# Masking the scale of Relu by expert, one sum for both halves, and turning the combine weights earlier

## The chip, the cores and the metric

The kernel runs on one core of a Trainium2 chip. The metric is the device time of one execution in microseconds (us), lower is better; a profiled execution has a span, and its time is a little longer than the span.

## The reference

An attention with a learned relative bias feeds a soft mixture of experts. Cut to what matters (the bias only named):

```python
# attention: 8 batches, 8 heads, 576 positions, head size 64, bias from a small MLP of log distances
attn = softmax(q @ k.T / 8 + bias) @ v            # -> x: 4608 tokens x 512
# soft MoE: 8 experts, 4 slots each (32 slots), hidden size 1024
logits = x @ phi                                  # 4608 x 32
d = softmax(logits, axis=tokens)
slot_input = (d.T @ x).reshape(8, 4, 512)
for e in range(8):
    slot_out[e] = relu(slot_input[e] @ w1[e]) @ w2[e]
c = softmax(logits, axis=slots)
out = c @ slot_out                                # 4608 x 512
```

## The kernel before, in words

**Main part.** 32 units (4 head pairs x 8 batches) go through attention. The order in which all steps are issued on all engines is a list written out by hand, `ORDER`: a token such as `Z/31` is step Z of unit 31. Each engine runs its own instructions in that order; semaphores make it wait for other engines. In the last eight units (24 to 31, one for each batch) each batch is also dispatched to the slots. Steps near the end of the list that matter here: `W` turns the exponentials and `wc` copies them into `ek`; `Z` multiplies them with the tokens (line 776) and `zc` (line 782) adds that to `accs`, the sums of all slots; `dq` copies the logits out of PSUM; `C`, `cA`, `cB`, `cC` make the combine weights of a batch, which are kept in `ck`; `F2` (line 826) and `F3` gather earlier sums. `cB/30` and `cB/31` are the two exponentials at line 750.

**The tail.** When the list is done, the code below `with tc.manual_schedule()` runs in program order. `turn_slots` transposes `accs` (line 971) and copies it to `sT` (line 973). `first(j)`, j = 0 to 7, multiplies it with w1 (line 986): Q = j // 4 is a half of four experts, which lie in four groups of 32 partitions, and within a group all 32 slots are computed, of which four are the expert's own. `hidden(Q)` applies Relu with the scale `stS` (1 / sum of the softmax), `turn_hidden(Q)` transposes the result to `hT` (line 1000). `stack(q)` transposes the combine weights of four batches to `cT` (line 1012) and those of the last 64 positions to `cR` (line 1015). `second(k, Q)` multiplies with w2 (line 1030) for k, one of four columns of 128 outputs. `gather_slots(k)` picks each expert's own four slots with the 0/1 matrix `sel`, one product for each Q (line 1042), and copies them to `sst` (line 1046). `put(k, q)` and `put_rest(k)` multiply with the combine weights (line 1063), copy the result from PSUM with ACT and DVE at once (line 377, tiles `ob`) and send it out (lines 1072 and 1079).

**PSUM.** There are eight banks. `Banks(w, n)` takes one bank (w = 1) or an aligned pair (w = 2) and gives it back after n calls of `read`, in program order: a pair is the one given back longest ago; a single bank is by preference one whose neighbour is taken, then the one given back longest ago. The new owner's products then wait for the old owner's copies. Each `put` and `put_rest` takes two pairs.

**Transfers.** All go through SP's queue in program order. `refetch` loads w2 tiles (512 KB each) into space that `first` has read.

## Time and profile before

| | |
|---|---|
| median of three runs | 580.82 us (578.47 to 581.24) |
| profiled execution | 579.62 us, span 577.8 us |
| PE, DVE, ACT, POOL busy | 547.1, 453.5, 458.4, 217.8 us |
| mean granted TensorE clock | 0.991 |
| HBM read, written | 81.25 MB, 27.41 MB |
| weight transfers | 62 of 512 KB (and 4 of 256 KB) |
| output transfers | 16 of 512 KB, 4 of 256 KB |

Busy times are of one core over the whole span. The lines of the profile have L and a line number of the kernel; `out<-in` are its tiles. Lines of the chain have start, length, engine and work; lines of the timeline add, in brackets, how long the engine had idled and who released it.

### The profile page before, as it was taken

How to read it: one execution, taken by the hardware profiler on the slowest of the kernel's cores; microseconds unless marked ns; L12 is line 12 of the kernel's file. 1: busy time of each engine (PE TensorE's matmuls, PEld its weight loads, DVE VectorE, ACT ScalarE, POOL GpSimd, SP SyncE). 2: the span in 40 equal slices, each digit the busy share in tenths (PEclk: the TensorE clock that was granted, in tenths of full speed). 3: DMA queues.
4: the chain of work that ended last, by engine and by line, in shares of the span. 5: the costliest groups of instructions: out<-in, count | busy, mean ns of one | idle time of the engine just before them, and what ended most of it. 6: DMA issues, size and time to landing. Idle time of an engine off the chain costs nothing.

```text
span 577.8 us, 19444 instructions
## 1 busy us (share of the span) xinstructions
PE 547.1 (95%) x7435; PEld 355.3 (61%) x7435; DVE 453.5 (78%) x1806; ACT 458.4 (79%) x955; POOL 217.8 (38%) x308
## 2 busy tenths in 40 slices
PE   5989899999999999999999999999999999989983
PEld 3445566667766666666776666667665666643762
DVE  7998778778889788787788888888897889862333
ACT  6979899988888998988988889888879788531233
POOL 4000445555545545555545544555334333400000
PEclk9999799999999999999999999999999999999998
DMA  5598613154865253868423256531453443699988
GB/s 159 213 310 297 187 64 105 62 161 143 294 182 188 90 177 120 288 190 290 157 88 102 85 187 170 179 104 43 137 186 123 124 169 118 245 392 408 404 336 329
DMA packets 43869, 109.91 MB, mean 190 GB/s; under 512 B 8448, under 2 KB 8576, under 8 KB 43776
## 3 DMA queue, kind: packets, MB, share of 16 engines
q1 hardware_dynamic: 43776, 108.67, 54.4%
q8 instruction: 58, 0.95, 0.7%
q14 instruction: 35, 0.29, 0.2%
HBM read 81.25 MB, written 27.41 MB: 188 GB/s over the span
## 4 chain that ended last, share of the span: by engine, by line
PE 67%; DVE 10%; ACT 9%; DMA 5%; issue 4%; POOL 2%; SPq 1%; DVEq 0%; ACTq 0%; POOLq 0%
PE ps L439 18%; PE ps L547 16%; PE ps L423 14%; DVE y L459 5%; ACT y L468 4%; PE ps L444 3%; DMA xo<-xs 3%; PE ps L557 3%; PE ps L1030 3%; PE ps L911 3%; PE ps L986 2%; ACT f L900 2%; POOL y L374 2%; DMA bias_m<-e 2%; ACT e L921 1%
## 5 line engine op out<-in xcount | busy, mean ns | idle before, releaser
L374 POOL TENSOR_SCALAR y<-y,sm 128x576 f32<-128x576 f32 x288 | 210.4, 746 | 274.1 <-DVE sm L476 218.3
L468 ACT ACTIVATE y<-y,mn 128x576 f32<-128x576 f32 x288 | 220.8, 770 | 21.2 <-DVE mn L459 16.0
L439 PE MATMUL ps<-qk 64*128 64x288 f32 x1024 | 161.1, 424 | 0.7 <-DVE ck L739 0.3
L377 ACT COPY at<-ps 128x1024 f32<-128x1024 f32 (+2 forms) x151 | 132.1, 895 | 22.1 <-PE ps L423 18.0
L547 PE MATMUL ps<-at,v 128*64 128x320 f32 (+1 forms) x1024 | 133.7, 410 | 0.2 <-ACT y L468 0.2
L459 DVE CUSTOM_DVE_ANT_0 y<-ps,bm,mn 128x288 f32<-128x288 f32 x256 | 123.4, 512 | 8.7 <-PE ps L439 3.4
L423 PEld LDWEIGHTS ps<-ident,y 64*128 64x128 f32 x2592 | 100.2, 139 | 43.4 <-POOL y L374 17.7
L459 DVE CUSTOM_DVE_ANT_0 y<-ps,bm 128x288 f32<-128x288 f32 x256 | 108.2, 453 | 15.1 <-PE ps L439 8.9
L423 PE MATMUL ps<-ident,y 64*128 64x64 f32 x2592 | 113.5, 227 | 3.3 <-DVE mn L459 1.0
L439 PEld LDWEIGHTS ps<-qk 64*128 64x128 f32 x1024 | 100.9, 188 | 18.6 <-DVE mn L459 3.2
L547 PEld LDWEIGHTS ps<-at,v 128*64 128x64 f32 x1024 | 69.9, 137 | 54.5 <-DVE mn L459 6.5
L468 ACT ACTIVATION_READ_ACCUMULATOR y<-y,mn 128x1 f32 x288 | 54.8, 190 | 0.0
L475 DVE TENSOR_SCALAR sm<-sm 128x2 f32<-128x2 f32 x144 | 36.2, 251 | 20.7 <-ACT y L468 20.3
L911 PE MATMUL ps<-f,wbd 128*32 128x79 f32 (+44 forms) x640 | 44.0, 404 | 6.8 <-DVE f L902 4.0
L902 DVE TENSOR_SCALAR f<-tabs,scl,nb 128x560 f32<-128x560 f32 (+17 forms) x106 | 45.9, 506 | 3.1 <-ACT f L900 1.5
L459 DVE DVE_READ_ACCUMULATOR2_ANT mn<- 128x1 f32 x576 | 47.6, 83 | 0.0
L911 PEld LDWEIGHTS ps<-f,wbd 128*32 128x32 f32 x640 | 22.0, 113 | 29.2 <-issue 10.5
L377 DVE COPY at<-ps 128x1024 f32<-128x1024 f32 (+2 forms) x41 | 31.2, 763 | 5.5 <-PE ps L423 4.4
L900 ACT ACTIVATE f<-tabs,cols,scl 128x432 f32<-128x432 f32 (+15 forms) x38 | 26.4, 748 | 2.5 <-DMA bias_m<-e 2.5
L476 DVE RECIPROCAL sm<-sm 128x2 f32<-128x2 f32 x144 | 23.8, 166 | 4.9
L921 ACT ACTIVATE e<-ps,bcon 128x591 f32<-128x591 f32 x36 | 25.8, 762 | 1.1 <-PE ps L911 1.1
L557 PE MATMUL ps<-at,v 64*64 64x320 f32 x128 | 23.9, 448 | 0.0
(150 smaller groups left out, 433.1 us busy)
## 6 DMA issues: line engine op xcount, KB each, us to landing
wt<-in_moe_w_dram SPq DMA_DIRECT2D x62, 512.0 KB, 6.9
qk<-in_qk_dram SPq DMA_DIRECT2D x32, 576.0 KB, 4.0
bias_m<-e SPq DMA_DIRECT2D x32, 295.5 KB, 3.6
v<-in_v_dram SPq DMA_DIRECT2D x32, 288.0 KB, 4.4
out_dram<-ob SPq DMA_DIRECT2D x16, 512.0 KB, 4.0
xs<-xts SPq DMA_DIRECT2D x24, 288.0 KB, 3.6
xo<-xs SPq DMA_DIRECT2D x8, 864.0 KB, 5.1
bm<-bias_m SPq DMA_DIRECT2D x16, 288.0 KB, 4.2
```

Of the source, the lines that this page charges most:

```text
L374: nc.gpsimd.tensor_scalar(out=out, in0=y, scalar1=r, scalar2=1.0, op0=ALU.mult, op1=ALU.mult)
L377: (nc.vector.tensor_copy if eng else nc.scalar.copy)(out=out, in_=in_)
L423: nc.tensor.matmul(out, src[rs], ident[rs, rs], is_transpose=True, start=True, stop=True, tile_position=(64 * r, 0))
L439: nc.tensor.matmul(pss[hh].t[:, 0:HALF], x[rs, S + p * P:S + (p + 1) * P], x[rs, k0:k0 + HALF], start=True, stop=True, tile_position=(64 * ...
L459: nc.vector.tensor_tensor_reduce(out=d["y", p][:, hs], in0=d["ps", p, n][hh].read()[:, 0:HALF], in1=biases[hp][p][:, hs], scale=-QS, scala ...
L468: nc.scalar.activation(out=y, in_=y, func=AF.Exp, bias=d["mn", p][:, 2 + hh:3 + hh], scale=-1.0, accum_out=d["sm", p][:, hh:hh + 1])
L475: nc.vector.tensor_scalar(out=r, in0=r, scalar1=1e-9, scalar2=None, op0=ALU.add)
L547: nc.tensor.matmul(po.t[o:o + 64, 0:wide[c]], d["v"][:, 64 * (4 * hh + i):64 * (4 * hh + i) + 64], main[:, :, 4 * hh + i, :], start=i == 0 ...
L557: nc.tensor.matmul(d["po", c].t[o:o + 64, 0:wide[c]], d["v"][rs, 512:576], keys[c][rs], start=False, stop=True, tile_position=(64 * hh, o))
L900: nc.scalar.activation(out=f, in_=tabs[:, 0:n], func=AF.Relu, bias=cols[:, 1:2], scale=sc)
L902: nc.vector.tensor_scalar(out=f, in0=tabs[:, 0:n], scalar1=sc, scalar2=nb1[:, 0:1], op0=ALU.mult, op1=ALU.max)
L911: nc.tensor.matmul(pb.t[32 * t:32 * t + 32, a // 512, a % 512:a % 512 + c1 - c0], wbd, x, start=True, stop=True, tile_position=(0, 32 * t))
```

## The change

- `turn_slots` makes `own`: `stS` times a 0/1 column for each Q, which is 1 where a row is a slot of the expert of its group. `hidden` uses it as Relu's scale, so that all other rows become 0.
- `second(k, 0)` and `second(k, 1)` then add into the same PSUM sums, and DVE copies them once for each k. `sel` loses its two halves, and `gather_slots` has one product.
- The sums and the gathered slots get a pair of banks of their own (`Banks(2, 99)`), one bank each, and are never given back. The gathered slots go into the second half of `so`.
- `stack` becomes a function of a list of batches. Six batches are turned as steps `k0/31` and `k1/31` in the list, ahead of and behind `Z/31`, and the last two behind `first(0)`. Each takes a single bank, and all copies are ACT's. `cT` is now two tiles.
- `second(k + 2, 0)` is written at the end of the loop, which is the same order as before.

The list gains two tokens; the rest of its diff is line breaks:

```diff
-... J8/30 F2/30 Z/31 F3/30 cC/31 d3/31 wat0/31 wqk0/31 wxo/31 zc/31 cB/30 wxk/31 cC/30
+... J8/30 F2/30 k0/31+ Z/31 k1/31+ F3/30 cC/31 d3/31 wat0/31 wqk0/31 wxo/31 zc/31 cB/30 wxk/31 cC/30
```

The rest:

```diff
-        sel = ends["sel"] = xp.tile([P, 2, P], F32, name="sel", tag="et2")
-        for Q in range(2):
-            nc.vector.tensor_scalar(out=sel[:, Q]..., scalar1=rowm[:, Q:Q + 1], ...)
+        sel = ends["sel"] = xp.tile([P, P], F32, name="sel", tag="et2")
+        nc.vector.tensor_copy(out=sel..., in_=rsum.unsqueeze(1).to_broadcast([P, 4, 32]))
+        own = ends["own"] = smp.tile([P, 2], F32, name="own", tag="se")
+        nc.vector.tensor_scalar(out=own, in0=rowm, scalar1=stS, scalar2=None, op0=ALU.mult)
...
-        nc.scalar.activation(out=hS[:, 0], in_=ends["h", Q].read()[:, 0], func=AF.Relu, scale=stS)
+        nc.scalar.activation(out=hS[:, 0], in_=ends["h", Q].read()[:, 0], func=AF.Relu, scale=ends["own"][:, Q:Q + 1])
...
+    def stack(turned, small):
+        if "cT" not in ends:
+            ends["cT"] = [xp.tile([P, 5, P], F32, name="cT", tag="lp")]
+        elif len(ends["cT"]) == 1:
+            ends["cT"].append(xp.tile([P, 5, P], F32, name="cT", tag="et"))
+            ends["cR"] = xp.tile([P, 2, 64], F32, name="cR", tag="acc")
+        h = Banks(1)
+        n = len(turned) * P
+        for i, b in enumerate(turned):
+            nc.tensor.transpose(out=h.t[:, i * P:(i + 1) * P], in_=ck[:, b, 0:4]..., identity=ident)
+        for q in small:
+            for i in range(4):
+                nc.tensor.matmul(h.t[32 * i:32 * i + 32, n:n + 64], ck[0:64, 4 * q + i, 4, :], ident[0:64, 0:64], ...)
+        h.read()
+        nc.scalar.copy(out=cT(turned[0], len(turned)), in_=h.t[:, 0:n]...)
+        for q in small:
+            nc.scalar.copy(out=ends["cR"][:, q], in_=h.t[:, n:n + 64])
+    step(U - 1, "k0", lambda _: stack((0, 1, 2, 3), ()))
+    step(U - 1, "k1", lambda _: stack((4, 5), (0,)))
...
     def second(k, Q, parts=(0, 1)):
-        if Q == 0:
-            ends["o", k] = Banks(1, 2)
+        if k == Q == 0:
+            ends["o"] = Banks(2, 99)
...
-        po = ends["o", k].t[:, P * Q:P * Q + P]
+        po = ends["o"].t[:, 0, P * k:P * k + P]
...
-                                     start=fq == 0 and x == 0, stop=fq == 1 and x == 3, tile_position=(0, 32 * g))
-        if parts[-1] == 1:
-            ends["o", k].read()
-            cp(Q == 0, ends["so"][:, Q, P * k:P * k + P], po)
+                                     start=Q == 0 and fq == 0 and x == 0, stop=Q == 1 and fq == 1 and x == 3,
+                                     tile_position=(0, 32 * g))
+        if Q == 1 and parts[-1] == 1:
+            nc.vector.tensor_copy(out=ends["so"][:, 0, P * k:P * k + P], in_=po)
     def gather_slots(k):
-        h = Banks(1)
-        pf = h.t[:, 0:P]
+        pf = ends["o"].t[:, 1, P * k:P * k + P]
         cs = slice(P * k, P * k + P)
-        for Q in range(2):
-            nc.tensor.matmul(pf, ends["sel"][:, Q], ends["so"][:, Q, cs], start=Q == 0, stop=Q == 1)
...
-        nc.scalar.copy(out=ends["sst"][:, cs], in_=pf)
+        nc.tensor.matmul(pf, ends["sel"], ends["so"][:, 0, cs], start=True, stop=True)
+        nc.scalar.copy(out=ends["so"][:, 1, cs], in_=pf)
...
         for j in range(4):
             first(j)
+            if j == 0:
+                stack((6, 7), (1,))
             refetch(*range(4 * j, 4 * j + (4 if j < 3 else 2)))
...
         turn_hidden(1)
-        stack(0)
-        second(0, 1)
-        stack(1)
+        second(0, 1, (0,))
+        second(0, 1, (1,))
+        second(1, 0)
         for k in range(4):
-            if k < 3:
-                second(k + 1, 0)
             gather_slots(k)
...
             put_rest(k)
+            if k < 2:
+                second(k + 2, 0)
```

## The prediction

> **What bounds the kernel now.** I read the page first, then stretches of the tail (the table of busy times by window), then the chain that ended last, and then the single rows of the tail in the timeline and the sync queue. The tail is where the edit lies, so the first question is what sets its end.

> ```profile
> span 577.8 us, 19444 instructions
> DMA  5598613154865253868423256531453443699988
> ...
> 502.00:554.60 52.60, 48.56 (x812) 28.13 (x807) 20.93 (x56) 13.56 (x33) 0.00 (x0) 1.00 1.01 397
> 554.60:557.00 2.40, 2.40 (x46) 1.71 (x46) 1.22 (x1) 1.28 (x2) 0.00 (x0) 1.00 0.34 126
> 557.00:562.60 5.60, 4.87 (x120) 3.60 (x112) 1.85 (x3) 1.55 (x3) 0.00 (x0) 1.00 1.02 398
> 562.60:565.00 2.40, 2.40 (x50) 1.85 (x48) 1.23 (x1) 1.30 (x3) 0.00 (x0) 1.00 0.22 82
> 565.00:576.60 11.60, 3.84 (x38) 1.96 (x30) 4.24 (x5) 3.74 (x6) 0.00 (x0) 0.92 1.01 398
> ```

> The columns after the stretch are PE, PEld, DVE, ACT and POOL busy, then the PE clock, the DMA share and GB/s. From 502 the DMA engines run full at about 398 GB/s, first on expert weights, then on outputs, with two holes: 2.40 us at 126 GB/s and 2.40 us at 82. Filled, they would save 2.40 x (1 - 126/398) = 1.64 and 2.40 x (1 - 82/398) = 1.91 us, 3.55 together. That is all this tail can give, because nothing ahead of k0 changes and no byte is taken away: 0.61% of the run. 0.5% is 2.9 us, about what a measurement of this kernel can tell from no change.

> ```profile
> 547.78 3.54 SPq L1072 DMA_DIRECT2D out_dram<-ob  x4
> 556.08 2.93 SPq L1072 DMA_DIRECT2D out_dram<-ob  x4
> 563.94 2.93 SPq L1072 DMA_DIRECT2D out_dram<-ob  x4
> 569.33 3.31 SPq L1072 DMA_DIRECT2D out_dram<-ob  x4
> ...
> out_dram<-ob SPq DMA_DIRECT2D x1, 512.0 KB, 2.6
> ```

> These are the first output issues of columns k = 0 to 3 in the sync queue, and (last line) the issue at 563.94, which lands 2.6 us later: 1.3 us of data, so 1.3 us ahead of it. The holes end when the outputs of k = 1 (556.08) and k = 2 (563.94) reach the queue. So the end of the kernel follows the issue of k = 2, and that follows TensorE, which the chain shows working back to back:

> ```profile
> 518.25 1.48 PE ps L776 x40
> 519.75 0.36 DVE accs L782
> 520.15 0.34 PE ps L971
> 520.51 0.27 ACT sT L973
> 520.83 10.51 PE ps L986 x96
> ...
> 537.68 1.02 PE ps L1000 x8
> 538.71 0.44 PE ps L1012 x4
> 539.14 0.24 PE ps L1015 x8
> ...
> 541.27 0.59 PE ps L1012 x4
> 541.86 0.25 PE ps L1015 x8
> ...
> 543.99 0.64 PE ps L1042 x4
> ```

> What counts is by how much later or earlier each put starts. I add shifts along this chain.

> **The change, part by part.**

> *The masked scale, sel and own.* The two Relu instructions keep their shapes and read another scalar column. The smaller sel and the new own are DVE work under the 10.51 us of first products, which need neither. Cost nothing; without that cover, well under 1 us.

> *k0 (turning four batches, ahead of Z/31).* By the rule of Banks (a lone bank whose neighbour is taken goes first) I followed the list by hand. F2/30 holds bank 3; k0 gets bank 2, which W/31 had; Z/31, which had it from W/31 before, now gets it from k0.

> ```profile
> 517.23 0.43 PE L826 MATMUL ps<-acc,rsum 128*32 128x128 f32 x8
> 517.65 0.56 ACT L750 ACTIVATE ck<-ck 128x160 f32<-128x160 f32 x2
> 517.77 0.33 DVE L377 COPY ek<-ps 128x160 f32<-128x160 f32 x1 [0.66 <-ACT xk L377]
> 538.30 0.59 ACT L377 COPY hT<-ps 128x512 f32<-128x512 f32 x1 [2.40 <-PE ps L1000]
> ```

> PE is idle from 517.66 to 518.25, which looks like room for the four transposes. But bank 2 is free only when the ek copy ends at 518.10; Z started 0.15 behind it. Now k0 starts there: four transposes 0.59 (to 518.84), a handoff of 0.02, the ACT copy of 128x512 (row: 0.59, to 519.45), 0.05 back, and Z at 519.50 instead of 518.25. **+1.25**. Lower end 0 (Z finds another bank and k0 fills the idle time), upper 1.5.

> *k1 (two batches and a quarter of rests, behind Z/31).* PE has it free while DVE adds accs, but ACT runs in order: k1's two copies and then cB/30, which ran at 517.9 before, now stand ahead of the copy of sT on which all first products wait.

> ```profile
> L377 ACT COPY ob<-ps 128x256 f32<-128x256 f32 x3 | 1.1, 378 | 0.0
> L1018 ACT COPY cR<-ps 128x64 f32<-128x64 f32 x2 | 0.4, 212 | 1.1 <-PE ps L1015 0.6 <-DVE hT L377 0.6
> ```

> Counted from the end of Z: two transposes (half of 0.59) and the small products (0.25) 0.55, handoff 0.02, copies 0.38 and 0.21, cB/30 0.28 (half of 0.56), sT 0.27, handoff 0.05: 1.76. Before it was 520.83 - 519.73 = 1.10. **+0.66**, between 0 and 0.9. The queue behind cB/30 on DVE (cC/30, four small operations) still ends under the first products.

> *stack((6, 7), (1,)) behind first(0).* Its weights are ready by then. Half of 0.59 and 0.25 on PE: **+0.55** (0.46 by the shorter row). The copies lie beside first products.

> *The old stacks leave.* The first took 0.44 + 0.24 = 0.69, but it covered ACT's copy of hT: that ends at 538.89, and the products that it feeds could start at 538.94, 0.23 behind the transposes. So 0.23 comes back as a wait: **-0.45**. The second took 0.84. It also kept column 1's sums, which now use the same bank, away from DVE's copy of column 0's:

> ```profile
> 537.80 0.29 DVE L377 COPY so<-ps 128x128 f32<-128x128 f32 x1 [1.05 <-PE ps L1030]
> 514.83 0.63 ACT L377 COPY lp<-ps 32x576 f32<-32x576 f32 x1 [4.41 <-DVE mb L657]
> ...
> 514.04 0.77 DVE mb L657
> ```

> No row shows PE writing a bank while another engine copies other columns of it. The nearest is dq/31 (second line): ACT needs nothing from DVE's minimum of the same banks, and yet idled 4.41 us and began 0.02 us after that had ended (514.81). So I let column 1 wait: 0.12 (537.68 to 537.80) + 0.29 + 0.05 = 0.46, and **-0.84 + 0.46 = -0.38**; the lower end is -0.84.

> [...]

> *One gather product instead of two.* Half of 0.64, four times: **-0.32** each, ahead of each put. The accumulation over Q costs no product; one copy of sums less per column was off the path.

> Sum at put(0, 0): 1.25 + 0.66 + 0.55 - 0.45 - 0.38 - 0.32 = **+1.31**.

> *The two own banks.* Before, second(2), second(3) and the last gather waited for a bank that an ACT copy was emptying:

> ```profile
> 549.05 0.40 PE L1063 MATMUL ps<-cR,sst 32*128 32x128 f32 x8
> 550.33 0.32 PE L1030 MATMUL ps<-wt,hT 128*32 128x128 f32 x4 [0.88 <-ACT ob L377]
> 558.19 0.43 PE L1030 MATMUL ps<-wt,hT 128*32 128x128 f32 x8 [0.73 <-ACT ob L377]
> ```

> That wait looks like the gain of the change, about 1 us a column. But two banks are now held to the end and three pairs are left. Followed by hand, put(k, 0) takes pairs A and B, put(k, 1) C and A, put_rest(k) B and C. Before, put_rest's second half had the pair of the sums and ran at once (0.40 for all eight). Now it needs C, which ACT is still emptying of put(k, 1): the same copy, the same end. PE is in order, so second(k+2) stands behind the same wait and behind half of put_rest: 0.20 later. I take **+0.20 per column**, not -1; the other end is a rival. With the gather's -0.32 each further column gains 0.12: put(1, 0) is at +1.19, put(2, 0) at **+1.07**.

> *What it meets in the queues.*

> ```profile
> SPq L882 <- PE ps L986: 2.9, 3, 2.2
> 541.32 0.33 SPq L882 DMA_DIRECT2D wt<-in_moe_w_dram  x1
> wt<-in_moe_w_dram SPq DMA_DIRECT2D x1, 512.0 KB, 10.1
> ```

> SP stops for first(0) to free weight space, 2.2 us at longest; first(0) ends 1.9 later, so 4.1. Transfers in flight last 10.1 us, so the stream does not run dry. The last weights land at 551.4. The output of column 0, issued at 547.78 + 1.31 = 549.1, has data from 550.4: no new hole. Column 2 is on the wire until 565 + 1.07 + 5.9 (four issues of 512 KB and one of 256, 2.36 MB, at 398 GB/s) = 572.0; column 3, issued near 570.3, still joins without a hole. So the end moves by 1.07: span 578.9, and with the 1.8 us around it 580.7 against this execution's own 579.62. The three timed runs had a median of 580.82 (578.47 to 581.24), 1.2 above the profiled one; the four together average 580.0. I state 580.0 + 1.1 = 581.1.

> **The rivals.**

> 1. *k0 and k1 really lie in idle time.* PE's 0.59 us of idle time ahead of Z speaks for it, the bank and ACT's order against. Without the 1.25 the shift is -0.2: 579.8. Without the 0.66 too, -0.8: 579.2. Both are within 0.5%.
> 2. *The own banks do what they say and the holes close.* Without the 1.91 of k0 and k1, with the whole 0.84 of the second stack and no wait at put_rest, put(1, 0) moves by 0.55 - 0.45 - 0.84 - 0.32 - 0.88 - 0.32 = -2.26, put(2, 0) by another 0.73 + 0.32, to -3.3, near the floor of 3.55: 576.7. The count of pairs speaks against it.
> 3. *Slower: the two own banks count as one resource.* Then each second's half behind a gather waits for ACT's copy of the gathered slots, 0.02 + 0.27 (as sT's) + 0.05 = 0.34, and up to 0.1 of drain: 0.44 three times ahead of put(2, 0), 1.3, so +2.4: 582.4. With k0, k1 at their upper ends (+0.5) it is 2.9 and decides. The other halves of pairs in the trace were used singly (second and gather had separate banks of one pair), which speaks against.
> 4. *The change does nothing.* Shifts cancel to within 0.5 us: 580.0 to 580.5, as like as the forecast for any reader of the time.

> **How the numbers follow.** The forecast (+0.5 to +1.8) 0.62; rivals 1 and 4 0.24; rival 2 0.05; rival 3 and other delays 0.09. Of the first two, next to all is within 0.5%: same 0.87. Faster by over 0.5% needs both holes nearly filled: 0.05. Slower 0.08. The range runs from rival 1 with a low set of runs (the shown runs scatter by 1.4 either way) to rival 3: 578.7 to 582.9.

> **What would show it.** In the changed profile: Z/31 (line 776, 764 there) begins behind an ACT copy into cT, near 519.5; first products start near 522.7; the products of second(1) idle some 0.4 us behind DVE's so; put_rest's products carry the wait for ACT ob that second(2) carried; the DMA table keeps both holes. I am wrong if put_rest runs without that wait, if Z starts at 518.3, or if the DMA share falls below 0.9 before 554.

## The result, and the profile after

The changed kernel takes 584.98 us (median of ten runs, 583.13 to 587.29) against 581.03 for the kernel before (ten runs beside it): ratio 1.0069, 95% interval 1.0043 to 1.0095. It is slower by 0.7%. I had put 581.1, a range to 582.9, and 0.08 on "slower". The profiled execution took 583.51, its span 581.7.

Stretches of the tail of the changed kernel, in the columns of the table in the prediction (the clock is third from the end):

```profile
span 581.7 us, 19421 instructions
...
514.40:517.80 3.40, 2.22 (x45) 1.59 (x45) 2.60 (x11) 2.47 (x6) 0.00 (x0) 0.98 1.04 389
517.80:528.00 10.20, 9.55 (x85) 3.70 (x89) 1.91 (x10) 1.37 (x6) 0.00 (x0) 0.50 0.87 328
528.00:549.00 21.00, 20.35 (x338) 10.72 (x334) 3.18 (x5) 2.82 (x5) 0.00 (x0) 1.00 1.01 400
549.00:553.00 4.00, 3.95 (x72) 2.21 (x64) 1.51 (x3) 1.24 (x2) 0.00 (x0) 1.00 0.35 132
553.00:558.00 5.00, 4.16 (x106) 3.41 (x110) 1.56 (x2) 1.33 (x3) 0.00 (x0) 1.00 0.98 384
558.00:561.00 3.00, 3.00 (x52) 1.66 (x44) 1.42 (x2) 1.19 (x2) 0.00 (x0) 1.00 0.36 138
561.00:566.00 5.00, 4.11 (x107) 3.41 (x110) 1.65 (x2) 1.39 (x3) 0.00 (x0) 1.00 1.02 397
566.00:569.00 3.00, 3.00 (x52) 1.66 (x44) 1.42 (x2) 1.13 (x2) 0.00 (x0) 1.00 0.33 123
```

The chain that ended last, from the copy of ek on:

```profile
516.06 0.34 DVE ek L365
...
516.44 0.67 PE ps L1003 x4
...
517.13 0.60 ACT cT L1009
...
517.77 2.52 PE ps L764 x40
...
522.33 3.64 PE ps L974 x16
525.98 0.62 PE ps L1003 x2
526.60 0.37 PE ps L1006 x8
526.97 9.19 PE ps L974 x80
...
540.75 1.75 PE ps L1028 x64
...
554.33 1.88 PE ps L1028 x64
...
562.38 1.88 PE ps L1028 x64
...
565.70 1.07 PE ps L1056 x8
```

The wait that I had forecast stands there as forecast: ek is copied, k0's transposes follow, ACT copies them, and only then Z (line 764) begins. But Z takes 2.52 us instead of 1.48, and the 16 products of first(0) 3.64 instead of a sixth of 10.51, 1.75. The same points in the kernel before:

```profile
535.93 1.75 PE ps L1030 x64
...
550.33 1.96 PE ps L1030 x64
...
561.79 1.07 PE ps L1063 x8
```

From the end of the ek copy to put(2, 0) it is 561.79 - 518.10 = 43.69 us before and 565.70 - 516.40 = 49.30 after, 5.61 more. In this execution the ek copy ended 1.70 earlier (the part ahead of it is the same code; its length differs between executions), and 5.61 - 1.70 = 3.91 is the whole difference of the spans, 581.7 - 577.8. So all of the loss lies between these two points. I had forecast 1.07 there.

### The profile page after: what moved, and what is told of

Same layout as the page of the kernel before. It is cut to its first block, busy times and chain, and to the rows that moved or that the text cites. A ratio compares the mean times of both kernels' runs of the same rounds, so it can differ in the third digit from the quotient of the medians.

```text
span 581.7 us, 19421 instructions
## 1 busy us (share of the span) xinstructions
PE 552.0 (95%) x7427; PEld 357.3 (61%) x7427; DVE 451.7 (78%) x1804; ACT 459.5 (79%) x954; POOL 217.1 (37%) x308
## 4 chain that ended last, share of the span: by engine, by line
PE 68%; ACT 10%; DVE 9%; DMA 5%; issue 3%; POOL 2%; SPq 1%; DVEq 0%; ACTq 0%; POOLq 0%
PE ps L427 18%; PE ps L535 17%; PE ps L411 14%; DVE y L447 5%; ACT y L456 3%; PE ps L974 3%; PE ps L545 3%; PE ps L1028 3%; PE ps L432 3%; ACT f L888 2%; PE ps L899 2%; PE ps L1056 2%; POOL y L362 2%; ACT e L909 1%; DMA bias_m<-e 1%
## 5 line engine op out<-in xcount | busy, mean ns | idle before, releaser
L899 PE MATMUL ps<-f,wbd 128*32 128x79 f32 (+45 forms) x640 | 43.7, 408 | 6.4 <-DVE f L890 3.9
L365 DVE COPY ob<-ps 128x1024 f32<-128x1024 f32 (+1 forms) x12 | 11.4, 957 | 19.1 <-PE ps L1056 12.9
## 6 DMA issues: line engine op xcount, KB each, us to landing
wt<-in_moe_w_dram SPq DMA_DIRECT2D x62, 512.0 KB, 6.2
out_dram<-ob SPq DMA_DIRECT2D x16, 512.0 KB, 3.5
```

The source lines that it names most:

```text
L365: (nc.vector.tensor_copy if eng else nc.scalar.copy)(out=out, in_=in_)
L899: nc.tensor.matmul(pb.t[32 * t:32 * t + 32, a // 512, a % 512:a % 512 + c1 - c0], wbd, x, start=True, stop=True, tile_position=(0, 32 * t))
```

## The experiments

Theory A: behind k0's hole TensorE loses half its clock (the 0.50 above), and the first products then run at half speed. Its rivals: B, the single sums and own banks lose the time; C, all handoffs up to sT together lose the clock; D, the waits are the loss and the clock is only seen beside it. "Half-clock time" is 2 x (1 - mean granted clock) x span of a run, the middle one of its runs given. Some of it lies away from the hole: in the profile of the kernel before 6.8 us from 62.7 on and 3.1 from 574.7 on, behind the last product, in that of the changed kernel 3.4 us from 63.7 on and 9.4 from 572.3 on. The ratios are against runs of the kernel before made beside each kernel, for the experiments on the same chip; the last column is the half-clock time of those runs, which differs between chips.

| kernel | median us | ratio, 95% interval | half-clock us | of the kernel before, same chip |
|---|---|---|---|---|
| before | 580.7 to 581.1 | 1 | 10.4 to 15.1 | |
| changed | 584.98 | 1.0069 (1.0043 to 1.0095) | 23.3 | |
| e1_old_stacks | 581.75 | 1.0029 (1.0004 to 1.0054) | 13.9 | 10.4 |
| e2_new_stacks | 585.55 | 1.0072 (1.0042 to 1.0101) | 23.4 | 10.4 |
| e3_k0_pair | 579.64 | 0.9993 (0.9971 to 1.0015) | 10.4 | 10.4 |
| e4_fill | 582.17 | 1.0026 (1.0003 to 1.0049) | 12.2 | 10.4 |
| e5_rest_late | 578.60 | 0.9964 (0.9943 to 0.9986) | 12.7 | 15.1 |
| e6_all | 577.33 | 0.9950 (0.9928 to 0.9972) | 15.0 | 15.1 |
| e7_before_rest | 579.86 | 0.9977 (0.9954 to 1.0001) | 12.7 | 15.1 |
| e8_hole | 585.01 | 1.0067 (1.0039 to 1.0094) | 17.5 | 15.1 |
| e9_hole_fill | 581.88 | 1.0018 (0.9994 to 1.0042) | 11.6 | 10.4 |
| e10_two_banks | 576.91 | 0.9941 (0.9916 to 0.9966) | 13.8 | 10.4 |

**Which part loses it: e1 and e2.** The change has two halves, which can be made one without the other.

```diff
 e1_old_stacks (on the changed kernel)
-k0/31, k1/31, stack((6, 7), (1,)) behind first(0)
+stack(0), stack(1) around second(0, 1), as before
 e2_new_stacks (on the kernel before)
+k0/31, k1/31, stack((6, 7), (1,)) behind first(0)
-stack(0), stack(1)
```

> The changed kernel with the turning of the combine weights put back where it was (two pairs of banks, ahead of and behind second(0, 1)); masked scale, single sums, one gather product and own banks stay. Theory A (TensorE idles behind the copy that k0 made, its clock is halved for some 10 us, and the first products run at half speed): the first products start 2.7 us behind the end of the ek copy as before, the clock stays at 1.00 until the last column, and the time is within 1.5 us of the kernel before (single sums and own banks cost or bring little, about +0.2 us a column). Theory B (the loss lies in the single sums and own banks, that is in the waits at put_rest): still 3 us or more slower than before, with a granted clock of 1.00 around the first products.

> The kernel before with only the new turning of the combine weights (k0 and k1 in the list, the last two batches behind first(0)); sums, gather and banks as before. Theory A: a stretch of about 10 us at half clock around the first products, 16 products of first(0) in 3.6 instead of 1.75 us, and the time 3 to 5 us above the kernel before. Theory B: the clock may fall or not, but the time is within 1.5 us of the kernel before.

The new place of the turning alone loses all of it (1.0072), with the half-clock time of the changed kernel. Its profile shows the same picture, Z and the 16 products of first(0) stretched, though less than expected (3.10 us for the 16 products, not 3.6):

```profile
520.91 2.47 PE ps L776 x40
...
525.42 3.10 PE ps L986 x16
```

Theory B falls as the main cause: single sums and own banks alone cost 0.29% (0.04 to 0.54), not 0.69%. They do cost something, 1.0 us by the medians, where I had expected about nothing.

**Hole or handoffs: e3.**

```diff
 e3_k0_pair (on the changed kernel)
-        h = Banks(1)
+        h = Banks(2 if len(turned) == 4 else 1)
```

> The changed kernel with one edit: k0 takes a pair of banks, so that Z/31 keeps bank 2 and does not wait for k0's copy. Theory A: Z starts 0.1 to 0.2 us behind the ek copy as before, TensorE has no hole there, the clock stays at 1.00 and the time falls by 3 to 4.5 us against the changed kernel, to within 1 us of the kernel before. Theory C (the clock falls because of all the handoffs up to sT, not of k0's hole alone): half clock is seen again, and no more than 1.3 us of the loss goes.

One edit of one bank takes 5.3 us off the median (4.4 us by the two ratios). Z no longer shares a bank with k0 (in the chain of e3_k0_pair the products of Z follow k0's transposes at once):

```profile
519.73 1.05 PE ps L1004 x4
520.78 2.33 PE ps L764 x40
```

Theory C falls. This profiled execution has a short stretch at half clock too (3.4 us from 519.4 on, Z takes 2.33), which began ahead of the hole's place. Others have one ahead of Z: that of e4 begins at 517.34, with Z at 520.43, and lasts 3.41 us; in e6 the clock is 0.76 between 515 and 516, with Z at 520.88; in e7 and e9 products shortly ahead of Z are stretched (line 638, 1.31 us for 16 in e7 and 1.04 for 12 in e9, against 1.15 for 16 in the kernel before). The middle of its runs has the half-clock time of the kernel before on that chip (10.4). That is why the verdict rests on the runs and not on one profile.

**Wait or clock: e4, e8 and e9.** e4 keeps the waits and fills them, e8 makes the hole alone, and e9 fills that.

```diff
 e4_fill (on the changed kernel; the transposes' results are not read)
+5 transposes of ident behind k0's, 4 behind turn_slots
 e8_hole (on the kernel before; the old stacks stay, the copy is not read)
+k0/31: four transposes in the bank that Z gets next, copied by ACT
 e9_hole_fill (on e8_hole)
+5 transposes of ident into another bank behind k0's four
```

> The changed kernel with nine more products of TensorE whose results nobody reads: five transposes of the identity while Z/31 waits for k0's copy and four while the first products wait for sT. All waits on the path stay. Theory A: the clock stays at 1.00, first(0) takes 1.75 us again, and the time is 2.5 to 4 us below the changed kernel, 0.5 to 2 us above the kernel before. Theory D (the waits on the path are the loss, the clock beside it only an indication): no change against the changed kernel.

> The kernel before with nothing but k0's hole: four batches are turned ahead of Z/31 in the bank that Z gets next, and ACT copies them to space that nobody reads; the old turning stays. Z starts 1.25 us later by the two handoffs. If a single hole of this size is enough to lose the clock (theory A in its narrow form), the half-clock time rises by 7 to 12 us and the time by 3 to 5 us. If the clock needs the longer series of waits up to sT (k0 and k1 together), it rises by the 1.0 to 1.5 us of the handoffs only.

> e8_hole with five transposes of the identity in the hole, into a bank that nobody reads; both handoffs stay on the path. Theory A (an idle TensorE loses the clock): the half-clock time goes back to that of the kernel before (12.7 us in the middle of its runs, 17.5 in e8_hole's), and of e8_hole's 3.9 us of loss 2 to 3 go; 0.8 to 1.8 us stay for the handoffs. If the wait itself is the loss: no change against e8_hole (585.0).

e4 keeps every wait and fills two of them. The time falls from 584.98 to 582.17 and the half-clock time to 12.2, against 23.4 for e2, which has the hole unfilled on the same chip. Theory D falls.

e8_hole is the kernel before plus one hole, and by the time it is as slow as the changed kernel (1.0067). Five transposes that nobody reads in that hole, with the same handoffs on the path, take 3.1 of its 3.9 us away (e9). What is left, 0.8 us in e9, is of the size of the handoffs (1.22 on the path). The chain of e9_hole_fill shows that they are there, and that Z behind them is at full speed:

```profile
518.52 0.34 DVE ek L377
...
518.89 0.67 PE ps L1024 x4
...
519.59 0.59 ACT cX L1028
...
520.23 1.48 PE ps L776 x40
...
522.88 10.51 PE ps L986 x96
```

The clock of e8 is less clean. I had expected its half-clock time to rise by 7 to 12 us; the middle run has 17.5 against 15.1 for the kernel before on that chip (the 12.7 in e9's expectation is the middle of the runs on two chips together). And its profiled execution had its half clock ahead of the hole (ek is copied at 522.83 there) and full clock behind it:

```profile
515.00:520.00 5.00, 4.86 (x64) 2.00 (x56) 3.18 (x9) 0.12 (x1) 0.00 (x0) 0.63 1.00 390
520.00:525.00 5.00, 3.27 (x63) 2.54 (x67) 3.82 (x13) 3.86 (x9) 0.00 (x0) 1.00 0.78 252
```

From the end of the ek copy to put(2, 0) that execution took 567.76 - 523.15 = 44.61 us, only 0.92 more than the kernel before, and the other 5 us that it is longer lie ahead of the hole. So the cause is shown for the changed kernel: by its profile and that of e2, in which Z behind the hole takes 2.52 and 2.47 us instead of 1.48, and by the runs of e3 and e4, which lose the wait or only its idle time and have the half-clock time back down. That k0's hole alone is enough rests on e8's time only: e9 ran on another chip, the intervals of the two just overlap, and no trace places what e8's runs lost beyond the handoffs.

**Where the expected use of the own banks went: e5 and e7.** In the changed kernel put_rest stands where second(k + 2) stood, behind the same ACT copy:

```profile
552.56 0.39 PE L1056 MATMUL ps<-cR,so 32*128 32x128 f32 x4
553.84 0.49 PE L1056 MATMUL ps<-cR,so 32*128 32x128 f32 x4 [0.89 <-ACT ob L365]
```

```diff
 e5_rest_late (on e3_k0_pair); e7_before_rest (the same order on the kernel before)
             put(k, 1)
-            put_rest(k)
             if k < 2:
                 second(k + 2, 0)
+            if k == 2:
+                gather_slots(3)
+            put_rest(k)
```

> The changed kernel with k0 on a pair of banks (as in e3_k0_pair), and second(k + 2, 0), and for the last column gather_slots(3), issued ahead of put_rest(k). If the wait for the ACT copy only moved from second to put_rest, and this copy is what keeps columns apart, TensorE does 1.9 us of products in that time instead of waiting: a column takes 7.0 instead of 8.05 us, the DMA holes ahead of columns 1 and 2 shrink from about 2 us each to under 1, and the time is 2 to 3 us below e3_k0_pair (579.6), that is 0.3 to 0.5% below the kernel before. If instead the copies themselves (ACT and DVE) bound a column, the column stays at 8 us and nothing is gained.

> The kernel before with one edit of order: second(k + 2, 0), and gather_slots(3), issued ahead of put_rest(k); nothing of the change. By the rule of banks second(k + 2) then gets a bank of the pair that the former sums left, and waits for nothing. If the single sums and own banks were not needed to get rid of that wait, this gains about 0.9 us a column as in e5_rest_late, 1.5 to 2.5 us below the kernel before. If the own banks are needed for it, no change.

The chain of e5_rest_late has no ACT copy between columns 1 and 2, and a column takes 556.75 - 549.71 = 7.04 us instead of 562.38 - 554.33 = 8.05:

```profile
549.71 1.89 PE ps L1029 x64
551.60 0.43 PE ps L1057 x8
552.03 0.42 PE ps L1039 x2
...
556.75 1.89 PE ps L1029 x64
```

So the wait was one of order. It goes in the kernel before as well (e7, a column takes 7.26 us), without own banks; there the gain is 0.23% with an interval that reaches 1, below what I had expected and not settled. e5 itself came out 1.0 us below e3 by the medians, not the 2 to 3 us expected. The intervals of e3 and e5 overlap; e5's lies wholly below 1.

**A version that beats both: e6 and e10.**

```diff
 e6_all (on e5_rest_late)
+k1's copies behind the copy of sT; stack((6, 7), (1,)) behind turn_hidden(1)
 e10_two_banks (on e6_all)
-        po = ends["o"].t[:, 0, P * k:P * k + P]
+        po = ends["o"].t[:, k % 2, P * k:P * k + P]
-        pf = ends["o"].t[:, 1, P * k:P * k + P]
+        pf = ends["o"].t[:, k % 2, P * (k ^ 1):P * (k ^ 1) + P]
```

> e5_rest_late with two further moves: k1's copies are issued behind the copy of sT, and the last two batches are turned behind turn_hidden(1), where second(0, 1) waits for a copy of hT, instead of behind first(0). By the working of the prediction this takes 0.66 (ACT's queue ahead of sT) and about 0.24 (cover of the hT copy) off the path, so 0.9 us less than e5_rest_late while the DMA holes have that much left; no more than about 0.5 if they are nearly filled. If TensorE's path no longer sets the end, no change.

> e6_all with the sums of even columns in one own bank and those of odd columns in the other (each column's gather product goes to the bank of its sums), so that second(1, 0) does not share a bank with DVE's copy of column 0. If two engines are kept off one bank at disjoint columns, as the prediction assumed, the 0.35 us of idle TensorE between second(0, 1) and second(1, 0) goes, and the time falls by up to 0.35 us against e6_all (577.3), less where the DMA holes are nearly filled. If that idle time has another cause, it stays.

Both are faster than the kernel before (0.9950 and 0.9941). The steps from e5 to e6 and from e6 to e10 are each within the uncertainty of the times, but the traces show them. In e6_all the copy of sT follows its transpose (line 959) at once, and second(0, 1) has cover; second(1, 0) still waits for DVE:

```profile
522.92 0.27 PE ps L959
...
523.22 0.28 ACT sT L961
...
541.88 1.93 PE ps L1035 x64
543.80 0.03 DVEq L1040
...
543.88 0.30 DVE so L1040
...
544.23 1.96 PE ps L1035 x64
```

With sums in alternate banks (e10_two_banks) the same two products run as one piece:

```profile
538.68 3.63 PE ps L1035 x128
```

The idle time between them (543.81 to 544.23, 0.42 us in this chain where the expectation had 0.35) is gone, and the two take 3.63 us instead of 546.19 - 541.88 = 4.31. So it was the shared bank, at columns that no one else touched. What ends it in e6_all is DVE's copy: second(1, 0) begins 0.05 us behind its end (544.18 to 544.23). Whether the two could run side by side in one bank no run shows.

## Why the prediction was wrong

**Step by step, most of it held.** From the ek copy to Z: +1.25 forecast, 1.37 - 0.15 = 1.22 measured. From Z's end to the first products, at full clock (e4_fill): 1.76 forecast, 523.62 - 521.96 = 1.66 measured. The old stacks: -0.45 forecast for the first, and 543.76 - 542.50 = 1.26 against 1.71 is -0.45; -0.38 for the second, -0.34 measured. The wait moved from second to put_rest, and the waits on the path are those that follow from the banks worked out by hand.

```profile
521.95 0.37 PE ps L1003 x2
...
523.62 1.92 PE ps L974 x16
...
542.50 0.60 PE ps L988 x4
...
543.76 2.00 PE ps L1028 x64
...
545.78 0.30 DVE so L1033
...
546.13 1.95 PE ps L1028 x64
```

(The first two lines are e4_fill's chain, the others the changed kernel's.)

**The step that failed is the one where I priced the hole by its length.** "+1.25, lower end 0, upper 1.5" took every product behind the hole at its duration before. From the ek copy to second(0, 0) it is 540.75 - 516.40 = 24.35 us, against 535.93 - 518.10 = 17.83 before: +6.52, where k0, k1 and the last batches were put at 2.46. The missing 4.06 is the clock. Row by row, against the same work at full clock: Z 2.52 instead of 1.48, the time from there to the first products 2.04 instead of 1.66, the 16 products of first(0) 3.64 instead of 1.75, the last batches 0.99 instead of 0.62 (e4_fill), and the 80 products behind them 9.19 instead of 8.76, 4.11 in all. My two sides for that cost left it out, although the table in the prediction has a clock column: its rows showed 1.00 wherever PE was busy, and 0.92 in the last one, where PE was idle for most of the time.

Those that run to the end of a span aside, the stretches at half clock in the traces last 3.4 us (e3 from 519.4 on, e4 from 517.3), 6.8 (the kernel before, from 62.7) and 10.2 (the changed kernel, from 517.7). In the 3.40 us ahead of the longest PE was busy for 2.22 us by the profile, not idle, and the clock came back only after 10.2 us in which it was busy for 94%. The kernel before had PE busy for 2.81 of 3.40 us at the same place (516.10 to 519.50), and its clock stayed at 1.00. Which waits cost the clock these traces do not show, and the page alone would not have given the loss.

**"The stream does not run dry" failed with it.** I had SP wait 4.1 us for first(0). It waited 4.8, and 2.7 more for Z, whose space it also needs, and the DMA share fell to 0.87 between 517.8 and 528, below the 0.9 that I had named as a sign of being wrong:

```profile
SPq L870 <- PE ps L974: 7.0, 4, 4.8
...
SPq L870 <- PE ps L764: 2.7, 1, 2.7
```

**Two terms were mis-sized.** One gather product of two saves 0.22 (0.42 instead of 0.64), not 0.32, and the waiting half of put_rest costs 0.49, not 0.20. A column so takes 8.05 us against 558.19 - 550.33 = 7.86, +0.19 where I had -0.12. In e1's trace the way from Z to put(2, 0) is 43.94 us against 43.54, 0.40 more; the rest of its 1.0 us no trace places. Rival 3 had the right side, but not its mechanism: nothing waits for both own banks (the gather products of column 0 end at 548.50, and the half of second behind them begins there), and no run shows its 0.1 us of drain: in the changed kernel DVE's copy so begins 0.02 us behind the products that it reads (545.76 to 545.78).

## What to carry to other kernels

A wait of TensorE is not always priced by its length alone: in the changed kernel a wait of 0.66 us was followed by a loss of 4 us beyond the forecast, and filling it and the next wait with products that nobody reads won 2.8 back. Before moving work "into idle time", follow which buffer it takes and who gets that buffer next; one bank made the difference between 1.007 and 0.999. A buffer of one's own removes a wait only if nothing behind it needs the buffer that is still being emptied; otherwise reorder first (the own banks left a wait of 0.89 us for ob, and the new order took a column from 8.05 to 7.04 us).

## What the runs showed of the hardware

- The busy share of TensorE by the profile does not tell by itself whether the clock is lost. In the changed kernel 2.22 us of work in 3.40 was followed by 10.2 us at half clock, though no idle time of PE in the 10 us ahead of it was longer than 0.82 us. In e4_fill 2.71 us of work in 3.41 was followed by 3.41 us at half clock (first two lines); in e8_hole 2.24 us in 3.41 was followed by full clock (last two lines). What decides between the two, these runs do not tell.

```profile
513.93:517.34 3.41, 2.71 (x66) 2.30 (x62) 3.18 (x8) 2.42 (x6) 0.00 (x0) 1.00 1.02 393
517.34:520.75 3.41, 3.14 (x26) 2.34 (x29) 1.69 (x8) 1.33 (x3) 0.00 (x0) 0.50 1.05 405
...
522.08:525.49 3.41, 2.24 (x49) 1.55 (x47) 1.77 (x9) 1.78 (x4) 0.00 (x0) 1.00 0.93 320
525.49:528.90 3.41, 2.52 (x32) 0.84 (x29) 1.87 (x9) 0.27 (x1) 0.00 (x0) 1.00 1.02 401
```

- The half-clock time differs between runs of one kernel, and with it the time: over the 88 runs of the kernel before beside e1 to e10 it goes from 6.9 to 23.3 us, and the two go together with a correlation of 0.80, 0.34 us of time for each us at half clock. Its middle differs between chips too (10.4, 15.1 and 10.4 us), so half-clock times are best compared on one chip.
